# LN2's output behind evacuations, a Wo inside MLP2, and two more groups with all 18 pairs of W2 rows in seven products

## The chip, the cores and the metric

The kernel runs on one core of a Trainium2 chip. The metric is device time in microseconds, the median of three runs; for the kernel before it is 359.16 us (359.07 to 359.28). The engines are called as in the profile: PE (matmuls; PEld is its weight loads), DVE (vector), ACT (scalar and activation), POOL (GpSimd) and SP (here it only issues transfers).

## The reference

One transformer block over 2048 tokens of width D = 576, in bf16. The attention is local: each token looks at W = 8 positions with a step of 2, in 32 heads of 18 columns. The MLP is 4608 wide.

```python
def _A_ref(x, wqkv, wo):
    W, dil = 8, 2
    q, k, v = qkv[0], qkv[1], qkv[2]          # of x @ wqkv, in 32 heads
    idx = pos[:, None] - off[None, :]         # off = arange(W) * dil
    mask = idx >= 0
    logits = jnp.einsum("bhsd,bhswd->bhsw", q, kg) * scale
    logits = jnp.where(mask[None, None, :, :], logits, -1e9)
    attn = _softmax(logits, axis=-1)
    o = jnp.einsum("bhsw,bhswd->bhsd", attn, vg)
    return o @ wo

def _B_ref(x, w1, b1, w2, b2):
    y = _layernorm(x, axis=-1)
    h = _gelu(jnp.einsum("bsd,df->bsf", y, w1) + b1)
    return jnp.einsum("bsf,fd->bsd", h, w2) + b2

h = x + _A_ref(_layernorm(x, axis=-1), A_wqkv, A_wo)
h2 = h + _B_ref(_layernorm(h, axis=-1), B_w1, B_b1, B_w2, B_b2)
```

## The kernel before, in words

**Tiles and stages.** The tokens are 16 tiles of 128 rows (token = 16 * row + tile), so that a tile's window lies in tiles of the same parity. First comes LN1 and QKV for all tiles, in 24 "visits" of two products each (the loop over `qd`). A visit works on 64 partitions at a time: phase 0 of each product in it, then phase 1 of each, each followed by an evacuation from PSUM on ACT (`qkv_duo`, L316). Three PSUM pairs take turns for these products. Then the tiles go through the rest as eight groups of two (`GROUPS`, here group 0 to 7; the loop over `k`). A group's step has MLP1 (four visits; gelu on ACT, L580, into `h_all`), then MLP2, and around it the Wo, LN2 and attention of later groups: `c, d` are the two tiles of the next group, `e, f` those of the group behind it.

**Order.** The order on each engine is the order in which the program is written (`manual_schedule`): nothing is moved by a scheduler. Lists of functions say what is put where: `after` and `between` (by visit, behind its evacuations), `m1` (ahead of a visit of MLP1), `ia`, `ib` (ahead of a row of MLP2 in groups 0 and 1) and `x` (at a named step of MLP2 in groups 2 to 7).

**Attention** is DVE's: `att_qk_a` (L346, QK products), four additions (L355), `att_max`, the exponential on ACT (`att_exp`, L389), `att_den`, `att_pv_a` (L403, PV products) and its sums (L409, L410). Its output goes back into `q_all`; SP stores it (`dma_out`, `td`) and reads it back turned as `oT` (L441), the Wo's operand. `halo` reloads one tile's rows of K or V shifted by one row, between the tiles.

**LN2.** `ln2_h` (L469, DVE) adds x to Wo's result in PSUM, `ln2_act` computes mean and variance on ACT (L491 to L493), a power on POOL (L494) gives the reciprocal root, `ln2_send` writes the output (L174), and SP stores it and reads it back turned as `hnT` (L510), MLP1's operand. Group 0's two tiles do it inside QKV: statistics on DVE, `ln2_rstd` on POOL (L161), `ln2_norm` on ACT (L535, L174), `h_tail` on POOL, `tr_h` on PE with a cast on ACT (L553).

**MLP2.** Groups 0 and 1 run 36 rows of W2 in two halves of 288 columns for each tile (`mlp2`, L599). Groups 2 to 7 take the two tiles and a pair of rows as a 2 by 2 product of blocks and run it in seven products instead of eight (`mlp2_fast`, `PRODUCTS`, L689). There are 18 pairs (`NM`). The seven need sums of h (`h_sums`, L669: s0 to s3, of 12 pairs at once and of the others behind) and of W2 (`w2_sums`, L659, once). Groups 2 to 5 do so for 16 pairs and run pairs 16 and 17 in eight products (`plain`); groups 6 and 7 run all 18 in seven. The order of steps is a list:

```python
if rows < NM:
    steps = ["wo", "hc", (1, all_), "b", "h", "e", (7, lo), (2, all_), (6, all_), "6", "7", "d", "11", (7, hi), "rest", "in",
              (5, all_), "f", "exp", (4, all_), "21", "22", "o1", "4", (3, all_), "12", "o0", "3"]
```

A tuple is a product over pairs; "b", "d" and "f" are copies from bank to bank on ACT (L776); "o1" are two additions on DVE (L720) that empty two banks, of which MLP1 of the next group uses the first for its second product; the other names run the functions of `x` under that name. `ln2_h` of `c` stands in "hc", that of `d` at the head of "h".

**Where sums lie.** Sums that don't fit in place stand in rows of `q_all`, `x_all` and the K and V rings that are free by then: `t_slot` for W2, `s_slot` for h. The second ring is free only from group 6 on.

Of the kernel before, what the change touches and what calls it, by code (L numbers as in the profile page):

```python
# [11 lines left out]
BF16 = mybir.dt.bfloat16  # L12
# [5 lines left out]
def kernel(  # L18
# [216 lines left out]

    def visit(makes, hook=None, between=(), late=None, apart=False):
# [17 lines left out]
        for n in range(len(makes) + (late is not None)):  # L254
            if late is not None and n == len(makes) - 1:
                first(late)
# [361 lines left out]
    def t_slot(t, m0, m1):  # L618
        if t == 2:
            return w2_block(0, 1, m0, m1).bitcast(F16)  # L620
        i = (0, 1, None, 2)[t]
        if m0 >= 16:
            return ring_blocks(1, (2 * i + m0 - 16) * HALF, m1 - m0, HALF)
        if i == 2 and m0 < 16:
            return ring_blocks(0, RING_T + m0 * HALF, m1 - m0, HALF)
        part = 0 if m1 <= 8 else 1 if m1 <= 12 else 2
        rows, j0 = ((x_all, (1, 9, 13)[part]), (q_all, (4, 12, 0)[part]))[i]
        m = m0 - (0, 8, 12)[part]
        j = j0 + 2 * (m // 2)
# [6 lines left out]
    spare = [False]  # L636
    RING_T = 3 * SR * P

    def s_slot(t, m0, m1):
# [5 lines left out]
        if not ring1_free[0]:  # L645
            rows, j = ((q_all, 15), (x_all, 10), (x_all, 8))[i] if spare[0] else (q_all, 15 - 2 * i)
            return rows[:, j, (m0 - SR) * P:(m1 - SR) * P].bitcast(F16).rearrange("p (m c) -> p m c", c=P)
        return ring_blocks(1, 6 * HALF + (i * (NM - SR) + m0 - SR) * P, m1 - m0, P)

# [57 lines left out]
    def mlp2_fast(g, rows, tags, wo, hooks):  # L707
        last, summed = wo is None, rows < NM
        q, p, r, s = tags
# [50 lines left out]
        }  # L760
        if rows < NM:
            steps = ["wo", "hc", (1, all_), "b", "h", "e", (7, lo), (2, all_), (6, all_), "6", "7", "d", "11", (7, hi), "rest", "in",
# [38 lines left out]
    with tc.manual_schedule(engines={ENG.PE, ENG.Activation, ENG.DVE, ENG.SP, ENG.Pool}):  # L801
# [132 lines left out]
        for v, fns in ((2, [(load_w1, 0)]), (3, [(load_w1, 1)]), (4, [(load_w1, 2)]), (6, [(load_wo, [0])]), (8, [(load_wo, [1, 2])]),  # L934
# [68 lines left out]

        def mlp1(grp, plan, ahead, between, late=None):
            for v, duos in enumerate(plan):
                call(ahead.get(v, ()))
                visit([mlp1_duo(grp, us, tag) for us, tag in duos], None, between.get(v, ()), late if v == 3 else None)

# [18 lines left out]

        ROWS = {6: NM, 7: NM}
        p, q, r, s = "ABDC"

        gelu_table()
        for k, g in enumerate(GROUPS):
            c, d = GROUPS[k + 1] if k + 1 < len(GROUPS) else (None, None)
            e, f = GROUPS[k + 2] if k + 2 < len(GROUPS) else (None, None)
            m1, mid, ia, ib, late_wo = {0: []}, {}, {}, {}, None
            if k in (1, 2):
# [7 lines left out]
            if k == 0:  # L1044
# [11 lines left out]
            elif k == 1:  # L1056
                m1[0] += [c_(att_pv_sum, d), c_(send_o, d), c_(halo, d, 2)]
                m1[1] += [c_(att_qk_a, e), c_(halo, e, 1), c_(read_o, d), c_(att_qk_b, e, 0), c_(halos, 7)]
                m1[3] += [c_(out_store, GROUPS[0][0]), c_(att_qk_a, f), c_(halo, f, 1), c_(att_qk_add, f, ((0, 0, 9), (0, 0, 4)))]
                ia[0] = [c_(wo_visit, (c, "B"), (d, "C")), c_(ln2_pair, c, d), c_(att_qk_b, f, 1, 2), c_(att_max, (e, f)),  # L1060
                         c_(exps, e, f), c_(w2_sums, 0, 8, (0, 1)), c_(w2_sums, 8, 12, (0, 1)), c_(att_den, e, f)]
                ia[2] = [c_(pv_sum, e), c_(dma_tr_o, e), c_(reload_x, GROUPS[4])]
                ib[0] = [c_(finish_out, g[0]), c_(out_sum, g[0])]
            if k < 2:
                mlp1(g, mlp1_plan(p, q, r, s, (s, r, p) if k else (r, s, p)), m1, mid, late_wo)
                mlp2_tile(g, 0, "D", ia)
                mlp2_tile(g, 1, "C", ib)
                continue
            rows = ROWS.get(k, 16)
            spare[0] = k == 2  # L1070
# [84 lines left out]
```

## Time and profile before

| | before |
|---|---|
| median of three runs | 359.16 us |
| profiled execution | 359.3 us, span 357.5 us |
| granted PE clock | 1.000 |
| busy in the span: PE, DVE, ACT, POOL | 351.9, 298.5, 235.8, 48.4 us |
| QKV ends, MLP1 of group 0 begins | 65.4 us |
| MLP1, Wo and MLP2 of group 3 | 177.7 to 213.6 us |
| MLP2 of group 4, of group 5, of group 6 begins | 233.6, 269.4, 305.2 us |

Times are from the start of the span. A timeline line has the start, the length, the engine, the line of the kernel, the operation, what it writes and reads, and the number of instructions that it merges; a bracket at its end is the idle time of the engine ahead of it and what ended that. A line of the waits has the waiter, what it waited for, the sum, the number of times and the longest. SPq is SP issuing a transfer, which lands later.

### The profile page before, as it was taken

How to read it: one execution, taken by the hardware profiler on the slowest of the kernel's cores; microseconds unless marked ns; L12 is line 12 of the kernel's file. 1: busy time of each engine (PE TensorE's matmuls, PEld its weight loads, DVE VectorE, ACT ScalarE, POOL GpSimd, SP SyncE). 2: the span in 40 equal slices, each digit the busy share in tenths (PEclk: the TensorE clock that was granted, in tenths of full speed). 3: DMA queues.
4: the chain of work that ended last, by engine and by line, in shares of the span. 5: the costliest groups of instructions: out<-in, count | busy, mean ns of one | idle time of the engine just before them, and what ended most of it. 6: DMA issues, size and time to landing. Idle time of an engine off the chain costs nothing.

```text
span 357.5 us, 11586 instructions
## 1 busy us (share of the span) xinstructions
PE 351.9 (98%) x4945; PEld 291.5 (82%) x4945; DVE 298.5 (84%) x428; ACT 235.8 (66%) x524; POOL 48.4 (14%) x63
## 2 busy tenths in 40 slices
PE   8999999999999999999999999999999999999996
PEld 4777987998788877887788778877887788778874
DVE  5999999999989999999999989998999998520431
ACT  4889756996647683678566856695669566706620
POOL 2241004000212020201200220022002200210000
PEclk9999999999999999999999999999999999999999
DMA  7997799954847584732553455345535253262001
GB/s 240 332 293 169 182 255 295 388 189 87 206 72 123 162 227 76 132 72 51 100 99 85 109 108 80 89 103 112 84 88 103 62 88 51 58 130 37 4 1 34
DMA packets 63492, 46.29 MB, mean 129 GB/s; under 512 B 32192, under 2 KB 61760, under 8 KB 63440
## 3 DMA queue, kind: packets, MB, share of 16 engines
q1 hardware_dynamic: 59472, 41.50, 44.1%
q0 software_dynamic: 3744, 3.84, 9.8%
q8 instruction: 38, 0.62, 0.7%
q10 hardware_dynamic: 224, 0.22, 0.3%
q14 instruction: 14, 0.11, 0.1%
HBM read 23.38 MB, written 12.42 MB: 100 GB/s over the span
## 4 chain that ended last, share of the span: by engine, by line
PE 51%; DVE 39%; ACT 3%; issue 2%; DMA 2%; SPq 1%; POOL 0%; DVEq 0%; POOLq 0%; ACTq 0%
PE pm L222 24%; PE po L689 24%; DVE prod L355 7%; DVE prod L346 6%; DVE prod L403 6%; DVE prod L409 5%; DVE ln_stats L148 3%; PE pw L222 3%; DMA x_all<-in_A_x_dram 1%; DVE den L397 1%; DVE h L469 1%; ACT h_all L580 1%; SPq L104 1%; DVE peak L370 1%; DVE q_all L410 1%
## 5 line engine op out<-in xcount | busy, mean ns | idle before, releaser
L222 PE MATMUL pm<-hnT,w_sb 64*128 64x256 bf16 x2304 | 143.0, 269 | 0.0
L580 ACT ACTIVATE h_all<-pm,b_sb 128x256 f16<-128x256 f32 (+1 forms) x288 | 108.6, 496 | 51.0 <-PE pm L222 50.4
L222 PEld LDWEIGHTS <-w_sb 64*128 64x128 bf16 x2304 | 113.2, 94 | 13.8 <-issue 1.6
L222 PE MATMUL pq<-wq_sb,xnT 64*128 64x288 bf16 x720 | 54.9, 283 | 1.0 <-ACT kv_ring L316 0.5
L689 PEld LDWEIGHTS <-h_all 128*128 128x128 f16 x464 | 44.7, 98 | 13.4 <-issue 1.8
L222 PEld LDWEIGHTS <-xnT 64*128 64x128 bf16 x864 | 43.7, 94 | 10.4 <-issue 1.4
L355 DVE TENSOR_TENSOR prod<-prod 128x2304 bf16<-128x2304 bf16 (+1 forms) x64 | 44.2, 691 | 2.1
L403 DVE TENSOR_TENSOR prod<-kv_ring,probs 128x4608 bf16<-128x4608 bf16 x16 | 40.9, 2558 | 0.9 <-DMA kv_ring<-kv_dram 0.4
L346 DVE TENSOR_TENSOR prod<-kv_ring,q_all 128x4608 bf16<-128x4608 bf16 x16 | 40.9, 2556 | 0.8 <-POOL ln_rstd L494 0.4
L222 PE MATMUL pm<-hnT,w1h_sb 64*128 64x256 bf16 x288 | 39.5, 269 | 0.0
L409 DVE TENSOR_TENSOR prod<-prod 128x2304 bf16<-128x2304 bf16 (+1 forms) x32 | 33.9, 1058 | 1.1
L689 PE MATMUL po<-w2a_sb,h_all 128*128 128x288 bf16 (+1 forms) x252 | 34.2, 286 | 0.2 <-ACT po L776 0.2
L599 PEld LDWEIGHTS <-h_all 128*128 128x128 bf16 x288 | 27.9, 98 | 7.9 <-issue 0.9
L689 PEld LDWEIGHTS <-kv_ring 128*128 128x128 f16 x252 | 24.7, 98 | 6.2
L599 PE MATMUL po<-w2a_sb,h_all 128*128 128x288 bf16 x224 | 28.5, 286 | 0.0
L789 POOL DMA_DIRECT2D x_all<-o_sb x12 | 10.7, 890 | 125.9 <-PE pw L222 54.4
L222 PE MATMUL pq<-wqh_sb,xnT 64*128 64x288 bf16 x144 | 27.6, 283 | 0.0
L494 POOL TENSOR_TENSOR ln_rstd<-ln_var,mhalf 128x1 f32<-128x1 f32 x13 | 10.3, 795 | 78.2 <-ACT ln_var L493 78.2
L669 DVE TENSOR_TENSOR kv_ring<-h_all 128x1536 f16<-128x1536 f16 (+3 forms) x9 | 6.8, 753 | 15.9 <-ACT h_all L580 15.9
L222 PE MATMUL pw<-wo_sb,oT 64*128 64x288 bf16 x256 | 19.5, 283 | 0.0
L161 POOL TENSOR_TENSOR ln_rstd<-ln_veps,mhalf 128x1 f32<-128x1 f32 (+2 forms) x14 | 13.1, 949 | 45.8 <-DVE ln_nmean L483 28.3
L689 PE MATMUL po<-w2b_sb,h_all 128*128 128x288 bf16 (+1 forms) x112 | 18.8, 286 | 0.2 <-DVE h_all L669 0.2
(121 smaller groups left out, 410.2 us busy)
## 6 DMA issues: line engine op xcount, KB each, us to landing
w_sb<-in_B_w_dram SPq DMA_DIRECT2D x6, 768.0 KB, 6.8
kv_ring<-kv_dram SPq DMA_DIRECT2D x28, 144.0 KB, 2.4
kv_dram<-kv_ring SPq DMA_DIRECT2D x13, 288.0 KB, 3.2
w2a_sb<-in_B_w_dram SPq DMA_DIRECT2D x3, 1008.0 KB, 9.7
x_all<-in_B_b_dram SPq DMA_DIRECT2D x15, 144.0 KB, 4.3
td<-q_all SPq DMA_DIRECT2D x14, 144.0 KB, 1.8
td<-hn SPq DMA_DIRECT2D x14, 144.0 KB, 1.8
x_all<-h POOLq DMA_DIRECT2D x14, 144.0 KB, 4.8
```

Source lines behind the costliest of these rows:

```text
L148: nc.vector.bn_stats(out=stats[:, i, c, :], in_=src[:, c * HALF:(c + 1) * HALF])
L161: nc.gpsimd.tensor_tensor(out=rstd[:], in0=veps[:], in1=mhalf[:].to_broadcast([P, n]), op=ALU.pow)
L222: last = nc.tensor.matmul(duo["g"][r ^ swap][i], lhsT=lhsT, rhs=rhs, start=(swap == 0 and i == 0 and kt == 0), stop=(swap == 1 and kt == K ...
L346: ins = nc.vector.tensor_tensor(out=prod[:], in0=k_ring[j % 2], in1=q_all[:, j, :].unsqueeze(1) .to_broadcast([P, W, D]), op=ALU.mult).ins
L355: nc.vector.tensor_tensor(out=prod[:, :, o * H:o * H + n], in0=prod[:, :, a * H:a * H + n], in1=prod[:, :, c * H:c * H + n], op=ALU.add)
L403: nc.vector.tensor_tensor(out=prod[:].rearrange("p w (d h) -> p w d h", h=H), in0=v_ring[j % 2].rearrange("p w (d h) -> p w d h", h=H), in ...
L409: nc.vector.tensor_tensor(out=prod[:, 0:n, :], in0=prod[:, 0:n, :], in1=prod[:, n:2 * n, :], op=ALU.add)
L494: ins = nc.gpsimd.tensor_tensor(out=rstd[:], in0=var[:], in1=mhalf[:], op=ALU.pow).ins
L580: pace[0] = nc.scalar.activation(out=hT(grp)[:, f, 0:N], in_=ps[:, r, i * N:(i + 1) * N], func=ACT.Gelu_apprx_tanh, bias=b1_sb[:, f:f + 1] ...
L599: nc.tensor.matmul(banks[half], lhsT=hT(grp)[:, f, i * P:(i + 1) * P], rhs=w2_rows(f)[:, half * HALF:(half + 1) * HALF], start=(f == 0), s ...
L689: nc.tensor.matmul(bank, lhsT=l, rhs=r, start=start, stop=stop, skip_group_check=True)
L789: nc.gpsimd.dma_start(out=x_of(j), in_=o_of.pop(j), accum_op=ALU.add)
```

## The change

It has five parts.

1. In QKV, the root, output and tail of LN2's first tile move by a visit or a place, so that on ACT two more evacuations stand ahead of its output; the exponential of group 1's first tile moves from visit 22 behind the evacuations of visit 23.
2. In group 0, the Wo of group 1's first tile is taken out of MLP1's last visit and put at the head of MLP2, cut in two by two rows of MLP2 (`fill`), as the second tile's Wo is; that one moves from row 19 to row 21.
3. In group 1, the second addition of a QK product moves behind the two `ln2_h`.
4. In groups 2 to 4 the sum s2 of 12 pairs moves from ahead of MLP2 into "hc", behind `ln2_h` of the first tile; in group 5 from the head of "h".
5. Groups 4 and 5 run all 18 pairs in seven products. The sums of W2 for pairs 16 and 17 move from group 6 to group 4 and into rows of `q_all`. The sums of h get other places: s1 of pairs 12 to 17 in a new buffer of `hnT` (so the turned LN2 output waits for its readers), s0 and s3 in `homes`. As written, s0 and s3 of pairs 16 and 17 lie in the first 512 columns of the row that holds s3 of pairs 12 to 15 and are written later, so product 3 of groups 4 and 5 reads other values there; the number, kind and order of instructions does not hang on that. The rows of x for group 6 are fetched in group 4 behind product 3 instead of in group 3.

```diff
@@ mlp2_fast
-        last, summed = wo is None, rows < NM
+        last, summed = wo is None, g not in GROUPS[6:]
...
-        if rows < NM:
+        if summed:
@@ t_slot, pairs 16 and 17
-            return ring_blocks(1, (2 * i + m0 - 16) * HALF, m1 - m0, HALF)
+            return q_all[:, 15 - 2 * i, (m0 - 16) * HALF:(m1 - 16) * HALF].bitcast(F16).rearrange("p (m c) -> p m c", c=HALF)
@@ s_slot
+    step_of, top = [0], [None]
+    homes = {2: ((q_all, 15), (x_all, 10), (x_all, 8)), 3: ((q_all, 15), (q_all, 13), (q_all, 11)), 4: ((q_all, 9), (x_all, 4), (x_all, 6)),
+             5: ((q_all, 9), (q_all, 5), (q_all, 7))}
...
-            rows, j = ((q_all, 15), (x_all, 10), (x_all, 8))[i] if spare[0] else (q_all, 15 - 2 * i)
+            if step_of[0] in FULL and t == 1:
+                rows, c = top[0][:].rearrange("p k c -> p (k c)"), 0
+            else:
+                rows, j = homes[step_of[0]][2 if m0 >= 16 else i]
+                rows, c = rows[:, j, :], (16 - SR - i) * P if m0 >= 16 else 0
...
+    def new_top():
+        top[0] = sb.tile([P, KT, 2 * P], BF16, tag="hnT", name="hnT")
@@ between, the visits of QKV
-            20: [c_(h_tail, A[0])],
-            19: {0: [c_(ln2_rstd, A[0])], 1: [c_(ln2_norm, A[0])]},
-            21: {0: [c_(ln2_rstd, A[1])], 1: [c_(ln2_norm, A[1])]},
-            22: {0: [c_(tr_h, A[0], "D")], 1: [c_(h_tail, A[1]), c_(att_exp, A[2])]},
+            19: [c_(ln2_rstd, A[0])],
+            20: {1: [c_(ln2_norm, A[0])]},
+            21: {0: [c_(h_tail, A[0]), c_(ln2_rstd, A[1])], 1: [c_(ln2_norm, A[1])]},
+            22: {0: [c_(tr_h, A[0], "D")], 1: [c_(h_tail, A[1])]},
+            23: {1: [c_(att_exp, A[2])]},
@@ group 0
-                late_wo = wo_duo(c, "B")
-                ia[0] = [c_(ln2_h, c), c_(ln2_act, c), c_(put_b2, c), c_(halos, 2), c_(ln2_send, c), c_(att_qk_b, e, 0)]
-                ia[19] = [lambda d=d: wo_visit((d, "A"), fill=True), c_(ln2_h, d), c_(ln2_act, d), c_(put_b2, d), c_(ln2_in, c),
+                ia[0] = [lambda c=c: wo_visit((c, "B"), fill=True), c_(ln2_h, c), c_(ln2_act, c), c_(put_b2, c), c_(halos, 2), c_(ln2_send, c), c_(att_qk_b, e, 0)]
+                ia[21] = [lambda d=d: wo_visit((d, "A"), fill=True), c_(ln2_h, d), c_(ln2_act, d), c_(put_b2, d), c_(ln2_in, c),
@@ group 1
-                m1[3] += [..., c_(att_qk_add, f, ((0, 0, 9), (0, 0, 4)))]
-                ia[0] = [c_(wo_visit, (c, "B"), (d, "C")), c_(ln2_pair, c, d), c_(att_qk_b, f, 1, 2), c_(att_max, (e, f)),
+                m1[3] += [..., c_(att_qk_add, f, ADDS[:1])]
+                ia[0] = [c_(wo_visit, (c, "B"), (d, "C")), c_(ln2_pair, c, d), c_(att_qk_b, f, 1, 1), c_(att_max, (e, f)),
@@ groups 2 to 7
-        ROWS = {6: NM, 7: NM}
+        FULL = (4, 5, 6, 7)
...
-                early = (0,) if k == 5 else (0, 2)
-                m1[3] += [c_(h_sums, 0, min(rows, SR), early)]
-                if k == 5:
-                    x["h"] += [c_(h_sums, 0, SR, (2,)), c_(h_sums, 0, SR, (1, 3))]
-                else:
-                    x["h"] += [c_(h_sums, 0, SR, [t for t in range(4) if t not in early])]
-                x["h"] += [c_(h_sums, SR, rows)]
+                m1[3] += [c_(h_sums, 0, SR, (0,))]
+                x["hc"] += [c_(h_sums, 0, SR, (2,))]
+                x["h"] += [c_(h_sums, 0, SR, (1, 3))]
+                if k in FULL:
+                    x["h"] += [new_top]
+                x["h"] += [c_(h_sums, SR, 16)]
+                if k in FULL:
+                    x["h"] += [c_(w2_sums, 16, NM)] if k == FULL[0] else []
+                    x["h"] += [c_(h_sums, 16, NM)]
...
-                    m1[1].append(c_(w2_sums, 16, NM))
...
-            if k + 3 < len(GROUPS):
-                x["3" if k == 2 else "in"] += [c_(reload_x, GROUPS[k + 3])]
+            if k in (2, 4):
+                x["3"] += [c_(reload_x, GROUPS[5 if k == 2 else 6])]
+            if k == 4:
+                x["in"] += [c_(reload_x, GROUPS[7])]
```

More of the change, by code (lines that the diff above doesn't have):

```diff
@@ L234, in marker, with visit @@
         return nop
-    def visit(makes, hook=None, between=(), late=None, apart=False):
+    def visit(makes, hook=None, between=(), apart=False):
         duos, marks = [], []
@@ L253, in visit @@
             return
-        for n in range(len(makes) + (late is not None)):
-            if late is not None and n == len(makes) - 1:
-                first(late)
+        for n in range(len(makes)):
             phase(duos[n], 1, marks[n])
@@ L635 @@
     ring1_free = [False]
-    spare = [False]
+    step_of, top = [0], [None]
+    homes = {2: ((q_all, 15), (x_all, 10), (x_all, 8)), 3: ((q_all, 15), (q_all, 13), (q_all, 11)), 4: ((q_all, 9), (x_all, 4), (x_all, 6)),
+             5: ((q_all, 9), (q_all, 5), (q_all, 7))}
     RING_T = 3 * SR * P
@@ L645, in s_slot @@
         if not ring1_free[0]:
-            rows, j = ((q_all, 15), (x_all, 10), (x_all, 8))[i] if spare[0] else (q_all, 15 - 2 * i)
-            return rows[:, j, (m0 - SR) * P:(m1 - SR) * P].bitcast(F16).rearrange("p (m c) -> p m c", c=P)
-        return ring_blocks(1, 6 * HALF + (i * (NM - SR) + m0 - SR) * P, m1 - m0, P)
+            if step_of[0] in FULL and t == 1:
[3 more added lines that the diff above has]
+                rows, c = rows[:, j, :], (16 - SR - i) * P if m0 >= 16 else 0
+            return rows[:, (m0 - SR) * P - c:(m1 - SR) * P - c].bitcast(F16).rearrange("p (m c) -> p m c", c=P)
+        return ring_blocks(1, (i * (NM - SR) + m0 - SR) * P, m1 - m0, P)
+    def new_top():
+        top[0] = sb.tile([P, KT, 2 * P], BF16, tag="hnT", name="hnT")
     def h_block(odd, i, m0, m1):
@@ L1002, in mlp1_plan, with mlp1 @@
             return [[([2 * v + n], tag) for n, tag in enumerate(tags)] for v, tags in enumerate(((p, q), (r, s), (p, q), end))]
-        def mlp1(grp, plan, ahead, between, late=None):
+        def mlp1(grp, plan, ahead, between):
             for v, duos in enumerate(plan):
                 call(ahead.get(v, ()))
-                visit([mlp1_duo(grp, us, tag) for us, tag in duos], None, between.get(v, ()), late if v == 3 else None)
+                visit([mlp1_duo(grp, us, tag) for us, tag in duos], None, between.get(v, ()))
         def mlp2_tile(grp, i, tag, inserts):
@@ L1034 @@
             e, f = GROUPS[k + 2] if k + 2 < len(GROUPS) else (None, None)
-            m1, mid, ia, ib, late_wo = {0: []}, {}, {}, {}, None
+            m1, mid, ia, ib = {0: []}, {}, {}, {}
             if k in (1, 2):
@@ L1058 @@
                 m1[1] += [c_(att_qk_a, e), c_(halo, e, 1), c_(read_o, d), c_(att_qk_b, e, 0), c_(halos, 7)]
-                m1[3] += [c_(out_store, GROUPS[0][0]), c_(att_qk_a, f), c_(halo, f, 1), c_(att_qk_add, f, ((0, 0, 9), (0, 0, 4)))]
-                ia[0] = [c_(wo_visit, (c, "B"), (d, "C")), c_(ln2_pair, c, d), c_(att_qk_b, f, 1, 2), c_(att_max, (e, f)),
+                m1[3] += [c_(out_store, GROUPS[0][0]), c_(att_qk_a, f), c_(halo, f, 1), c_(att_qk_add, f, ADDS[:1])]
+                ia[0] = [c_(wo_visit, (c, "B"), (d, "C")), c_(ln2_pair, c, d), c_(att_qk_b, f, 1, 1), c_(att_max, (e, f)),
                          c_(exps, e, f), c_(w2_sums, 0, 8, (0, 1)), c_(w2_sums, 8, 12, (0, 1)), c_(att_den, e, f)]
@@ L1064 @@
             if k < 2:
-                mlp1(g, mlp1_plan(p, q, r, s, (s, r, p) if k else (r, s, p)), m1, mid, late_wo)
+                mlp1(g, mlp1_plan(p, q, r, s, (s, r, p) if k else (r, s, p)), m1, mid)
                 mlp2_tile(g, 0, "D", ia)
@@ L1068 @@
                 continue
-            rows = ROWS.get(k, 16)
-            spare[0] = k == 2
+            rows = NM if k in FULL else 16
+            step_of[0] = k
             x = {n: [] for n in ("hc", "h", "6", "7", "in", "exp", "4", "3")}
```

## The prediction

> **What bounds the kernel now.** I read the page's shares and chain first, then the waits of PE, the chain in order of time, and the timelines of the engines at each place that the change touches.
>
> ```profile
> PE 351.9 (98%) x4945; PEld 291.5 (82%) x4945; DVE 298.5 (84%) x428; ACT 235.8 (66%) x524; POOL 48.4 (14%) x63
> PE 51%; DVE 39%; ACT 3%; issue 2%; DMA 2%; SPq 1%; POOL 0%; DVEq 0%; POOLq 0%; ACTq 0%
> ```
>
> PE works nearly all the time and DVE almost as much. The waits of PE, all that the profile has of them behind the first microseconds:
>
> ```profile
> PE pq L222 <- ACT kv_ring L316: 0.5, 1, 0.5
> PE po L689 <- ACT po L776: 0.2, 1, 0.2
> ```
>
> From about 165 us the chain is PE alone. Its pieces (start, length) give the price of a group's MLP1, Wo and MLP2, with 128 and with 126 products:
>
> ```profile
> 213.58 17.79 PE pm L222 x324
> 231.37 2.21 PE pw L222 x36
> 233.58 15.79 PE po L689 x128
> ...
> 305.15 15.54 PE po L689 x126
> ```
>
> So the end moves by what PE's work and its stalls become, and DVE counts where something that PE needs comes late. DVE's timeline in groups 4 to 7 shows how little it has to spare; the bracket is idle time and what ended it:
>
> ```profile
> 232.08 0.96 DVE L669 TENSOR_TENSOR h_all<-h_all 128x1536 f16<-128x1536 f16 x1
> 233.13 1.42 DVE L469 TENSOR_TENSOR h<-pw,x_all 128x576 f32<-128x576 f32 x2
> 239.28 2.56 DVE L346 TENSOR_TENSOR prod<-kv_ring,q_all 128x4608 bf16<-128x4608 bf16 x1 [0.44 <-POOL ln_rstd L494]
> 247.01 0.95 DVE L720 TENSOR_TENSOR o_sb<-po,o_sb 128x288 f32<-128x288 f32 x2 [0.44 <-PE po L689]
> 260.30 0.46 DVE L410 TENSOR_TENSOR q_all<-prod 128x576 bf16<-128x576 bf16 x1
> 268.91 1.42 DVE L469 TENSOR_TENSOR h<-pw,x_all 128x576 f32<-128x576 f32 x2 [1.08 <-PE pw L222]
> 296.85 0.45 DVE L659 TENSOR_TENSOR kv_ring<-w2b_sb 128x576 f16<-128x576 bf16 x1
> 342.02 0.29 DVE L669 TENSOR_TENSOR kv_ring<-h_all 128x256 f16<-128x256 f16 x1 [1.36 <-ACT h_all L580]
> ```
>
> The last things that PE waits for from DVE are the attention outputs: SP stores them and reads them back turned as oT for the Wo of the same group. SP's issues, the page's time to landing, and PE's second Wo in groups 5 and 6:
>
> ```profile
> 262.84 1.21 SPq L441 DMA_TRANSPOSE oT<-td  x1
> 298.94 1.21 SPq L441 DMA_TRANSPOSE oT<-td  x1
> oT<-td SPq DMA_TRANSPOSE x14, 2.9
> 267.60 0.65 PE L222 MATMUL pw<-wo_sb,oT 64*128 64x288 bf16 x8
> 303.39 0.65 PE L222 MATMUL pw<-wo_sb,oT 64*128 64x288 bf16 x8
> ```
>
> Landed at 262.84 + 2.9 = 265.7 and 298.94 + 2.9 = 301.8, the outputs lie ready 1.9 us and 1.6 us ahead of PE. That is the margin that a later DVE may use up.
>
> **The change part by part.**
>
> *LN2 output and exponential behind evacuations.* At 58.20 PE has two products left and would go on at 58.32; it goes on at 58.95, because ACT first waited 1.75 us for POOL's power (54.28 to 57.14), wrote LN2's output (0.29 + 0.87) and only then emptied the bank (58.27, 0.63). With two evacuations ahead of that output the bank is empty at about 57.6, and 0.63 us go. What is late next: the output of the second tile keeps its place, it hangs on DVE (h at 58.76, power until 61.61), so the evacuation behind it still ends at 63.37; PE's next user of that bank began at 63.51 and can begin at 63.42 at best. Of 0.63 us 0.09 are left. Then MLP1 began at 65.44, right behind the cast of hnT (64.69 to 65.39), which had the exponential (0.43) ahead; without it the cast can begin at 64.4, ends at 65.1, and PE begins at 65.16. Gain 0.28, which holds the 0.09. The exponential moves behind both evacuations (to about 66.2) and pushes the table load (1.28) by as much; the first gelu had 0.71 us of idle time ahead of it, and the softmax sum needs it at 70.5. Nothing.
>
> *Wo in MLP2.* The Wo of group 1's first tile stood inside MLP1's last visit with one change from its products on 64 rows to MLP2's on 128 (pw to po at 84.34). Now it is cut in two within MLP2, as the second tile's is: at 88.9 to 91.05 such a cut costs 0.17 into Wo and 0.16 out of it, start to start beyond the plain pace (0.0545 us a product on 64 rows by pairs, 0.122 on 128). The new cut adds one more way in, with 0.14 + 0.07, and one more way out, 0.16: +0.36. Bounds: nothing, if the array were free in between, and 0.69, twice the whole. I take 0.36, the row of the same cut. Its h on DVE starts at 87.5, behind a QK product; Wo is then done at about 85. The second tile's Wo moves two rows (four products, 0.49) later; h at 91.62 waits some 0.1 us, which DVE loses.
>
> *One addition less ahead of group 2's h's.* DVE's h's of 124.78 start about 0.5 us earlier and LN2 on ACT with them; the addition of 0.70 is done behind. The exponentials come sooner and DVE's idle 0.76 us at 133.6 goes.
>
> *h's ahead of sums.* In group 2, PE's 12 products from 163.36 would end in a next start at 164.83; it was 165.24, for the copy of a bank (164.79, 0.39) behind ACT's statistics, which waited 0.85 for h at 162.10. Now h goes ahead of a 0.96 us sum; ACT is then held by its own gelus until 162.04, the copy starts at 164.1, and 0.41 us go. The sum itself still comes at 162.7, where product 7 wants it at 163.4. In group 3 and 4 PE waits for nothing there, and DVE loses: between the first sum's end (232.04) and Wo's result (233.13) it did the second sum; now it idles there and does the sum behind h, a step of 0.87 us more. In group 3 an idle 0.90 ahead of o_sb at 211.23 covers this. In group 4 the next item uses that cover.
>
> *All 18 pairs in groups 4 and 5.* PE: 126 for 128 products, 15.79 − 15.54 = 0.25 a group, −0.50. DVE in group 4 does the four sums of W2 (296.85 to 298.65, steps 0.48 + 0.48 + 0.39 + 0.37 = 1.72; they leave group 6, where DVE waits anyway) and in both groups four sums of h of 0.29 (steps 0.33 + 0.21 + 0.20 + 0.21 = 0.95). Group 4: 0.87 + 1.72 + 0.95 = 3.54 more; of the idle 0.44 and 0.44 all but the usual 0.03 each, so 0.82, is used up: DVE ends the group 2.72 us late. Bounds for this lag: 1.5, if each sum cost the shortest step of its kind (4 x 0.37 + 4 x 0.20 - 0.82) and h's idle time did not arise, and 3.5, if no idle time were recovered; I take 2.72, as every step has its own row. Product 6 needs its last sums at 241.42 and gets them at about 241.1; MLP1's second bank is emptied at 250.2, when PE wants it: up to 0.08 lost.
>
> *The lag at PE.* Group 5's attention is DVE without a gap, so its second output ends at 260.76 + 2.72 = 263.48, is issued 2.08 later and lands 2.9 behind that, at 268.46. PE, 0.17 early by then (0.25 less 0.08), wants it at 267.43: a stall of 1.03. This covers the sum that product 7 needs (272.2). In group 5 h comes late too, at 266.95 + 2.72 + 0.92 = 270.59 for 268.91; with four small sums more DVE passes on 1.68 + 0.95 = 2.63 us into group 6, whose second output lands at 301.84 + 2.63 = 304.47. PE wants it at 303.39 − 0.17 + 1.03 − 0.25 = 304.00: 0.47 more. Behind it DVE idles 1.73 us (h at 304.70) and the lag is gone; the last two groups run as before. Stalls 0.08 + 1.03 + 0.47 = 1.58.
>
> *x reloads and POOL.* The rows of group 6 are fetched behind group 4's product 3 instead of in group 3. SP's next issues there wait for DVE anyway (252.83), and the rows are needed at 270: nothing, and if that cover were gone, the fetch's 3.6 us would delay the halo and add to the lag. The turned LN2 outputs now wait for product 6, at 241.7; SP issued them at 242.51.
>
> Sum: −0.28 + 0.36 − 0.41 − 0.50 + 1.58 = **+0.75 us**. The profiled execution took 359.3 (span 357.5, 1.8 around it), 0.14 above the median of 359.16; against the median the forecast is 359.9.
>
> **The rivals.**
>
> *The lag stays hidden (faster).* Place: oT of groups 5 and 6. If DVE's lag is below 1.6 us there, no output is late, and the sum is −0.28 + 0.36 − 0.41 − 0.50 = −0.83, 358.3. For it: 1.5 as the lower bound of the lag. Against it: the sums' rows vary by hundredths. It decides at 1.6 us.
>
> *A slow transfer falls on the late one (slower).* The oT of 262.84 took 4.6 us to land, where the median is 2.9; the margin hid it. With none, 4.6 − 2.9 = 1.7 go to PE in full: 361.6. The longest of the 14 took 4.9; two are exposed. In the window of 262 to 268 the instruction queue (q8) fetched its one 16 KB packet. [...]
>
> *The early gains don't come.* If the stalls at 58.95 and 165.24 only move on, +0.69 is left out: 360.6. For it: the first moves by my own working. I count it within the forecast's range.
>
> **How the numbers follow.** Forecast 0.55 (its own range 359.4 to 360.6), hidden lag 0.15, slow transfer 0.25, something else 0.05. A measurement of this kernel can tell about 0.2% (0.72 us) from no change. The forecast lies on that bound: 0.30 slower, 0.24 same, 0.01 faster. Hidden lag: 0.10 faster, 0.05 same. Slow transfer: slower. The rest: 0.03 slower, 0.02 same. Together 0.11, 0.31, 0.58. Range 358.4 to 361.7: from the hidden lag to the slow transfer.
>
> **What would show it.** A second Wo in groups 5 and 6 that starts 0.3 to 1.2 us behind its first, with PE waiting for oT; h of group 5 at 1.5 us or more behind its Wo; no wait at 58.95 and 165.24; the Wo of group 1 in two pieces; o_sb of group 4 some 2.7 us later than now. If DVE's lag in group 5 is under 1.6 us, or PE's Wo shows no wait there, the forecast is wrong.

## The result, and the profile after

The changed kernel takes 361.69 us in the median of 22 runs (359.62 to 364.46), the kernel before 359.16 (358.60 to 361.38, 22 runs): ratio 1.0058, 95% interval 1.0045 to 1.0071. It is slower, by 0.6%. Its times fall into two heaps: seven runs at 359.6 to 360.2, fifteen at 361.4 to 364.5. The profiled execution (360.0, span 358.2) is of the first heap; a second profile, shown below, is of the other.

The page of the changed kernel, busy times and chain:

```profile
PE 351.0 (98%) x4941; PEld 289.2 (81%) x4941; DVE 299.6 (84%) x436; ACT 235.8 (66%) x524; POOL 47.5 (13%) x63
...
q8 instruction: 38, 0.62, 0.8%
...
PE 70%; DVE 15%; DMA 6%; ACT 4%; SPq 2%; issue 2%; DVEq 0%; ACTq 0%
```

q8 is read here as the queue that brings PE's instructions: 38 blocks of 16 KB for 9,882 of them (PE and PEld, 4,941 each), of which the one near group 5's store comes at the same place of PE's program in all fourteen traces (see e5). PE has 0.9 us less work than before; DVE has 1.1 us more, and transfers have 6% of the chain for 2%. Behind QKV, PE's waits (waiter, cause: sum, times, longest) have two new lines:

```profile
PE pm L222 <- DMA hnT<-td: 0.8, 1, 0.8
...
PE pw L222 <- DMA oT<-td: 0.6, 1, 0.6
```

The first is ahead of group 5's MLP1, the second ahead of the second Wo of group 6; from start to start of PE's products they cost 0.91 and 0.76 us beyond the usual step. Against the profile of before:

| | forecast | profiled execution |
|---|---|---|
| PE ahead at the end of group 3's MLP2 (212.80 for 213.30) | -0.33 | -0.50 |
| 126 for 128 products, groups 4 and 5 (15.54 each) | -0.50 | -0.50 |
| wait for LN2's turned output, group 4's step | 0 | 0.91 |
| bank at 250.2; second Wo of group 5 | 0.08; 1.03 | 0; 0 |
| second Wo of group 6 | 0.47 | 0.76 |
| sum; span | +0.75 | +0.67; +0.7 |

Why LN2's output was late stands in SP's timeline, first of the kernel before, then of the changed one (start, length):

```profile
240.88 0.43 SPq L205 DMA_DIRECT2D td<-hn  x1
241.87 0.33 SPq L341 DMA_DIRECT2D kv_ring<-kv_dram  x1
242.51 2.52 SPq L510 DMA_TRANSPOSE hnT<-td  x2
```

```profile
240.36 0.43 SPq L205 DMA_DIRECT2D td<-hn  x1
244.37 0.33 SPq L339 DMA_DIRECT2D kv_ring<-kv_dram  x1
244.88 2.52 SPq L508 DMA_TRANSPOSE hnT<-td  x2
```

The stores went out earlier than before, but a refill of the K ring stands ahead of the turned reads in SP's queue. It waits until DVE's QK product has read the ring (SP waited 3.5 us for it, and issued the refill 0.03 us behind its end at 244.34), and DVE was late. DVE of the changed kernel:

```profile
241.79 2.55 DVE L344 TENSOR_TENSOR prod<-kv_ring,q_all 128x4608 bf16<-128x4608 bf16 x1
```

That is 2.51 us later than the 239.28 of before. The chain of the changed kernel at group 6 shows the other wait (start, length, what): store, turned read, Wo, each straight behind the one before.

```profile
299.49 1.54 DMA td<-q_all
...
301.11 2.93 DMA oT<-td
...
304.08 1.77 PE pw L222 x26
```

### The profile page after: what moved, and what is told of

Read it like the earlier page. It is cut to its first block, busy times and chain, and to the rows that moved or that the text cites. A ratio compares the mean times of both kernels' runs of the same rounds, so it can differ in the third digit from the quotient of the medians.

```text
span 358.2 us, 11596 instructions
## 1 busy us (share of the span) xinstructions
PE 351.0 (98%) x4941; PEld 289.2 (81%) x4941; DVE 299.6 (84%) x436; ACT 235.8 (66%) x524; POOL 47.5 (13%) x63
## 4 chain that ended last, share of the span: by engine, by line
PE 70%; DVE 15%; DMA 6%; ACT 4%; SPq 2%; issue 2%; DVEq 0%; ACTq 0%
PE pm L222 29%; PE po L696 16%; PE pq L222 11%; PE po L597 10%; PE pw L222 3%; DVE prod L353 2%; ACT h_all L578 2%; DVE prod L401 2%; DVE prod L344 2%; DVE prod L407 2%; DMA xnT<-xd 2%; DMA td<-q_all 2%; DMA x_all<-in_A_x_dram 1%; SPq L104 1%; DVE kv_ring L676 1%
## 5 line engine op out<-in xcount | busy, mean ns | idle before, releaser
L696 PEld LDWEIGHTS <-h_all 128*128 128x128 f16 x448 | 43.3, 98 | 12.6 <-issue 1.4
L222 PEld LDWEIGHTS <-xnT 64*128 64x128 bf16 x864 | 42.0, 94 | 12.3 <-issue 1.4
L783 ACT COPY po<-po 128x288 f32<-128x288 f32 x17 | 6.6, 386 | 18.8 <-PE po L696 18.8
```

The lines of the kernel that those rows point to most:

```text
L222: last = nc.tensor.matmul(duo["g"][r ^ swap][i], lhsT=lhsT, rhs=rhs, start=(swap == 0 and i == 0 and kt == 0), stop=(swap == 1 and kt == K ...
L696: nc.tensor.matmul(bank, lhsT=l, rhs=r, start=start, stop=stop, skip_group_check=True)
```

## The experiments

The kernel before took 359.07 to 359.19 us in the same sessions; a ratio is against it. W2's sums are those of `w2_sums`, s2 is the sum of 12 pairs that the change moved.

### e1_again: the other heap

The changed kernel, no edit.

> The changed kernel, unaltered, profiled a second time. Its 22 times fall into two heaps, seven at 359.6 to 360.2 us and fifteen at 361.4 to 364.5; the profile at hand (360.0) shows the short heap, with PE waiting 0.91 us for the turned LN2 output in group 4's step and 0.83 us for the second attention output of group 6. Theory 1, a slow transfer: a profile of the long heap shows the same waits and one of them some 2 us longer, by a landing of over 4 us where the short one has 2.4 to 3.7. Theory 2, DVE itself runs slower in the long heap (its instructions longer or with more gaps): then DVE's chain from 210 us on is some 2 us longer and every wait behind it grows. Theory 3, the start: the first transfers come 2 us later. If the run falls into the short heap the profile repeats the one at hand within 0.3 us.

361.62 us. PE's waits:

```profile
PE pw L222 <- DMA oT<-td: 2.6, 2, 1.7
...
PE pm L222 <- DMA hnT<-td: 0.7, 1, 0.7
```

Beyond the usual step they are 0.80 (LN2), 1.81 (Wo of group 5, where the short profile has none) and 1.09 (Wo of group 6). The chain at group 5's second output:

```profile
262.36 0.34 SPq L204
...
262.75 3.37 DMA td<-q_all
...
266.17 2.83 DMA oT<-td
...
269.05 1.03 PE pw L222 x13
```

The store took 3.37 us; the read behind it took its usual 2.8. The transfers from 263 to 267, in 40 slices of 0.1 us (busy share in tenths, then GB/s):

```profile
DMA  0069993636000000000001000000000000000000
GB/s 0 0 242 415 392 323 105 104 49 164 0 0 0 0 0 0 0 0 0 0 4 6 0 0 0 0 0 0 0 0 0 0 0 0 0 0 0 0 0 0
...
q8 instruction: 1, 0.02, 1.7%
```

The packets of the two stores run from 263.2, those of the small one (issued at 262.75) from 263.7. In the tenth slice one 16 KB block of instructions begins (the 164; it is booked at its start, 264.00, and took 1.07 us). Then nothing, and at 265.0 to 265.2 the last few small packets. Packet by packet: 120 of the small store's 128 had gone by 263.91, the other eight, a sixteenth of them where the profile counts 16 DMA engines, began at 265.05, when the block was through; which engine a packet took, the trace does not show. The short profile, 263.5 to 267.5:

```profile
DMA  0189974720000005000000000025477999732000
GB/s 0 69 311 380 380 265 99 107 28 0 0 0 0 0 0 164 0 0 0 0 0 0 0 0 0 0 51 125 118 164 179 259 243 225 172 62 42 0 0 0
```

Here the store is through at 264.39 and the block begins at 265.08, between the store and the turned read. So theory 1 holds, a transfer, though in the small store and not in the read; DVE's instructions around it have the same lengths in both (theory 2 falls), and up to group 5 the long execution is 0.44 us ahead (247.90 for 248.34), so theory 3 falls too.

### e2_sp_order: turned reads ahead of the refill

```diff
-                x["in"] = [c_(ln2_ins, c, d)] + x["in"]
+                if k == 4:
+                    x["7"].insert(1, c_(ln2_ins, c, d))
+                else:
+                    x["in"] = [c_(ln2_ins, c, d)] + x["in"]
```

> One edit to the changed kernel: in group 4's step SP issues the two turned reads of LN2's output ahead of the K ring's refill that waits for DVE's QK product (it ended at 244.34 us in the profile; the stores had landed at 241.94 and product 6 was over). Both theories say that the reads are issued at about 242.0 instead of 244.9, land by about 246.5, and PE's wait of 0.91 us ahead of group 5's MLP1 is gone. Theory A, DVE's chain sets the end from group 4 to 6: DVE's outputs come no sooner, PE arrives 0.9 us earlier at Wo of group 5 and waits some 0.3 us there (output landed at 267.69, PE would want it at 267.35), and the rest again at group 6 (landed at 304.04): the time stays at that of the changed kernel within 0.2 us. Theory B, the order on SP is the whole loss: the waits at Wo stay as they were and the time falls by 0.9 us, to 359.1 for a run like the profiled one. The rarer and the commoner heap of times (360 and 362) may change their shares: if the long heap comes from the late turned read, it is gone here and the median falls below 360.2.

362.29 us in six runs (361.46 to 362.52), ratio 1.0082 (1.0066 to 1.0097). SP's timeline and PE's largest wait:

```profile
241.67 2.52 SPq L508 DMA_TRANSPOSE hnT<-td  x2
244.29 0.53 SPq L339 DMA_DIRECT2D kv_ring<-kv_dram  x1
```

```profile
PE pw L222 <- DMA oT<-td: 2.1, 1, 2.1
```

The wait for LN2's output is gone, as both theories said, and nothing is won: PE comes sooner to Wo of group 5 and waits there. Theory B falls. Theory A had the time stay within 0.2 us, and it is 0.6 above; PE's granted clock, the page's row of 40 slices in tenths, shows what came on top:

```profile
PEclk9999999999999999999999999999998999999999
```

PE's step ahead of that Wo was 2.39 us. From 270.25 on the granted clock was 0.5 for 3.41 us; the rest of the Wo took 2.41 us for 1.69 and MLP2 16.46 for 15.54, so the stall cost 1.6 us more than its wait. (A further 0.4 us is a wait for POOL's markers in group 5's MLP1.) In e1_again a step of 1.94 us left the clock at 1.0.

In this profile, too, eight packets of the store stayed back until 265.38, when a block (264.45) was through; its record begins 0.43 us behind the last of the other 120, so the eight were late before it begins, which the block's record does not explain. No run was in the short heap.

### e3_s2_ahead, e7_no_w2_sums, e10_no_lag: less work on DVE in group 4

```diff
@@ e3: s2 of group 4 ahead of Wo again
-                m1[3] += [c_(h_sums, 0, SR, (0,))]
-                x["hc"] += [c_(h_sums, 0, SR, (2,))]
+                m1[3] += [c_(h_sums, 0, SR, (0, 2) if k == 4 else (0,))]
+                if k != 4:
+                    x["hc"] += [c_(h_sums, 0, SR, (2,))]
@@ e7: no W2's sums for pairs 16 and 17 (e10: both edits)
-                    x["h"] += [c_(w2_sums, 16, NM)] if k == FULL[0] else []
```

> One edit to the changed kernel: in group 4 alone the sum s2 of 12 pairs stands ahead of MLP2 again, as in the kernel before; it fills 0.96 of the 1.07 us in which DVE waited for Wo at 231.56. Theory A, DVE's chain sets the end: all that DVE does behind it comes 0.9 us earlier (the QK product at 240.9 instead of 241.79, the second output of group 6 landed at 303.1 instead of 304.04), PE's wait for the turned LN2 output falls from 0.91 to under 0.1 us, and the time falls by 0.9 us, to 359.1 for a run like the profiled one; PE's waits left are some 0.8 us, at Wo of group 6. Theory B, the lag of DVE counts for little and the order on SP for all: the time still falls by 0.9 us, but the wait at Wo of group 6 stays at 0.83 us with its output landed at 304.0. In group 4 the copy of a bank behind ACT's statistics may cost PE up to 0.1 us.

> The changed kernel with the four sums of W2 for pairs 16 and 17 left out altogether (products 4 to 7 of the last four groups read other values for these pairs), which takes 1.72 us of DVE out of group 4. Theory A, DVE's lag is what PE waits for: the waits of 0.91 us (turned LN2 output of group 4) and 0.83 us (second attention output of group 6) both go, and a short run takes 358.3 us; a block of instructions on the store of group 5's second output delays it to about 267.9 where PE wants it at 267.35, so a long run takes 358.9. Median 358.3 to 358.9. If instead the new buffer of s1 or the order on SP holds the turned LN2 output, the wait ahead of group 5's MLP1 stays at some 0.9 us and the time stays above 359.2.

> Both of DVE's additions that could be taken away alone: the sum s2 ahead of MLP2 in group 4 and the four sums of W2 left out altogether (products 4 to 7 of the last four groups read other values for pairs 16 and 17). DVE then has 0.95 us more in group 4 than with the first four parts alone, and 0.82 of idle time to take it. Each edit alone gave 360.28 and 359.18 us. If DVE's lag, and the blocks of instructions that fall on its late outputs, are all that part 5 loses, the 2 x 0.25 us of PE now show in full: no wait at group 5's MLP1 and at Wo of groups 5 and 6, 358.67 - 0.50 = 358.2 us. If a block of instructions still reaches the turned read of group 6 (it took 2.9 to 4.3 us so far), PE waits there for up to 0.5 us: 358.7. If part 5 costs something that isn't DVE's (the new homes, the later fetch of x), the time stays at 358.9 or more with a wait elsewhere.

| run | DVE's lag less by | median us (runs) | range | ratio, interval |
|---|---|---|---|---|
| e3_s2_ahead | 0.96 | 360.28 (12) | 358.51 to 361.69 | 1.0027, 1.0010 to 1.0044 |
| e7_no_w2_sums | 1.72 | 359.18 (12) | 358.36 to 361.59 | 1.0001, 0.9986 to 1.0017 |
| e10_no_lag | both | 359.44 (11) | 358.83 to 360.13 | 1.0010, 0.9998 to 1.0021 |

Each edit alone takes the wait for LN2's output away, with SP's order and the new buffer as they were: the lag of DVE made it (theory A). The profile of e3 was its fastest run, 358.51, and PE's waits behind QKV are down to Wo of group 6:

```profile
PE pw L222 <- DMA oT<-td: 0.5, 1, 0.5
```

What its other runs wait for, no profile shows. The medians don't follow the lag down. e7 lies 0.3 us above its expectation and e10 no lower than e7, where I expected 358.2 or, with a block on the read, 358.7. In e10 the chain at group 6 is

```profile
298.42 4.46 DMA oT<-td
...
302.93 0.29 PE pw L222
```

The read went out 2.7 us sooner than in the changed kernel, and took 4.46 us for 2.93. Of its 32 completion writes 30 were done by 300.82; a block began at 300.88, and the last two came at 301.82. In e7 the read was issued 0.81 us later than in e10 (299.23) and landed only 0.30 us later (303.18). PE's wait at this Wo, which e7 was to lose, was 1.26 us beyond the usual step in e7 and 0.97 in e10, for 0.76 in the changed kernel: PE came there sooner, the output did not. In e10 the landing (302.88) followed the last two writes, behind a block that comes with PE's own program, and of the 2.7 us by which the read went out sooner 1.16 were left (304.04 in the changed kernel).

### e5_block_later, e9_block_earlier, e13_no_lag_block_later: where the blocks fall

In all fourteen traces, q8's block near group 5's store comes when PE has begun 7,603 to 7,644 of its 9,900 instructions: a place in PE's program, give or take half a microsecond. These edits move that place and nothing behind the start.

```diff
@@ e5, and e13 (on top of e10)
-        for n in [512] * 8 + [P] * 8:
+        for n in [512] * 9:
...
-        for n in range(12):
+        for n in range(10):
@@ e9
-        for n in [512] * 8 + [P] * 8:
+        for n in [512] * 6 + [P] * 16:
```

> The changed kernel with 9 fewer warm-up products at the very start (9 of 512 columns instead of 8 of 512 and 8 of 128; 10 small ones instead of 12), which are 18 instructions of PE less, and nothing else. The traces so far: q8 fetches one 16 KB block of instructions per some 256 instructions of PE. In the long profile (361.6) the block began at 264.00, as the small second store of group 5's second attention output ended (120 of its 128 packets by 263.91); its last 8 packets started at 265.05, when the block was through, and the turned read behind it was issued at 266.17 instead of 264.81. In the short profile (360.0) the block began at 265.08, 0.69 us behind the store's end, and no packet was held. Theory C, the block on the store makes the long heap: 18 instructions fewer put the block some 0.5 us later against all else (256 instructions lasted 7.5 us there), past the store in nearly all runs; the long heap is gone or rare and the median falls from 361.7 to 359.9 to 360.6 (the block may touch the turned read of group 6, 0.5 us at most). Theory D, the heaps have another cause (the state of the chip, DVE): the times fall into the same two heaps, about two in three at 361.4 or more, median near 361.7.

> The other way: 6 warm-up products more (6 of 512 and 16 of 128 columns, about the same time), 12 instructions of PE more, so that each 16 KB block of instructions is fetched some 0.35 us earlier against all else. Theory C, the block on the store makes the long heap: the short heap needs the block to start more than 0.4 us behind the store's end, so it becomes rarer still, at most one run in six, and the median stays at 361.7 to 362.4. Theory D, another cause: seven of 22 in the short heap as before.

> The run with s2 ahead in group 4 and without W2's sums (359.44 us), with 18 instructions of PE fewer in the warm-up, so that each 16 KB block of instructions comes some 0.5 us later. There the block of 300.88 held the last two of the 32 completion writes of group 6's turned read (30 by 300.82, two at 301.82), which landed at 302.88, and PE waited 1.05 us in the fastest kind of run. Theory C: the block comes behind that read in most runs, the wait falls below 0.3 us and the time to 357.9 to 358.6, so that the 0.5 us of PE's fewer products show. Against it: that PE, with fewer products, meets the read of group 6 before it has landed whatever the block does; then the time stays at 359.2 or more, and the profile shows the wait with a landing of 2.9 us or less.

e5: 360.46 us in ten runs, eight of them at 360.2 to 360.7; ratio 1.0039 (1.0024 to 1.0054). That is within theory C's 359.9 to 360.6, though between the two heaps and not in the short one. The profiled one is the longest, 361.9. Its block comes at 266.20, behind the store's end at 265.13, and the store is free; but the next block lies on group 6's read, and the chain there is

```profile
301.60 4.35 DMA oT<-td
```

e9: 360.89 us in seven runs (360.49 to 362.02), ratio 1.0051 (1.0033 to 1.0069). None is in the short heap, as theory C said, but the median was to be 361.7 or more. In its profile the block (263.67) holds the store as in e1_again, and lets it go earlier, so that the store takes less:

```profile
262.68 2.98 DMA td<-q_all
```

These two ran one after the other on one chip, the 22 runs of the changed kernel at another time, so the shares of the heaps are best compared between the two. The step from e5 to e9 goes in the direction of theory C, and is smaller than it said: that packets stay back until a block is through is seen in the traces (eight of 128 in e1_again, e2 and e9), how much of the heaps it makes is in part argued.

e13: 359.78 us in twelve runs; eleven of 359.5 or more, one of 357.72; ratio 1.0021 (1.0005 to 1.0038). Neither expectation fits. The block still lies on the read's end: 30 of 32 completion writes by 301.74, the block at 301.90, two writes at 302.83, and the chain

```profile
299.46 4.47 DMA oT<-td
...
303.97 1.03 PE pw L222 x13
```

In e10 and here the block's record begins within 0.02 us of the read's last packet, though it was moved by 18 instructions. Whether the block itself queues behind the read's packets, so that half a microsecond doesn't part them, stays open. The one run at 357.72, 2 us below the rest, would be an execution in which they missed each other; it has no profile, so this is argued only.

### e4_parts1to4, e6_no_cut, e12_sums_only: the first four parts

```diff
@@ e4: groups 4 and 5 as before
-        FULL = (4, 5, 6, 7)
+        FULL = (6, 7)
@@ e6, on top of e4: Wo of group 1's first tile back in MLP1
-                ia[0] = [lambda c=c: wo_visit((c, "B"), fill=True), c_(ln2_h, c), ...]
-                ia[21] = [...]
+                late_wo = wo_duo(c, "B")
+                ia[0] = [c_(ln2_h, c), ...]
+                ia[19] = [...]
@@ e12, on top of e6: LN2 in QKV as before
-            19: [c_(ln2_rstd, A[0])],
-            20: {1: [c_(ln2_norm, A[0])]},
-            21: {0: [c_(h_tail, A[0]), c_(ln2_rstd, A[1])], 1: [c_(ln2_norm, A[1])]},
-            22: {0: [c_(tr_h, A[0], "D")], 1: [c_(h_tail, A[1])]},
-            23: {1: [c_(att_exp, A[2])]},
+            20: [c_(h_tail, A[0])],
+            19: {0: [c_(ln2_rstd, A[0])], 1: [c_(ln2_norm, A[0])]},
+            21: {0: [c_(ln2_rstd, A[1])], 1: [c_(ln2_norm, A[1])]},
+            22: {0: [c_(tr_h, A[0], "D")], 1: [c_(h_tail, A[1]), c_(att_exp, A[2])]},
```

> The changed kernel without its fifth part: groups 4 and 5 run 16 pairs in seven products and two in eight, and the sums of W2 for the last two pairs are back in group 6, in the second ring (only the later fetch of group 6's x stays). By the theory that the fifth part makes all the loss, DVE is late by no more than 0.1 us in group 4 (0.87 more work, 0.82 of idle time to take it), PE waits nowhere from 205 to 305 us, and PE stays as far ahead of the kernel before as it was at 212.8 us in the profile, 0.50 us: 358.8 for a profiled run, ratio about 0.9986, and the long heap is as rare as in the kernel before (4 of 22). By the rival, that the first four parts cost as well (the second addition of group 4's idle place, the cut Wo), the time is 359.2 or more. By my own earlier sum the first four parts are worth 0.28 - 0.36 + 0.41 = 0.33 us.

> The run with the first four parts only (358.67 us), with one edit: the Wo of group 1's first tile is back in MLP1's last visit, in one piece, and the second tile's Wo back at row 19. By my prediction's row the cut costs 0.36 us of changes between products on 64 and on 128 rows (in the profile of the changed kernel 0.155 + 0.098 + 0.07 + 0.155 at 83.5 to 84.7, of which the uncut one has 0.155): the time falls to 358.3. By the rival that DVE, which this Wo releases half a microsecond sooner, gains as much elsewhere, it stays at 358.7 within 0.15 us.

> The kernel before with the third and fourth part alone (the addition behind the h's of group 2, and h's ahead of the sum s2), and the later fetch of group 6's x. By my prediction's terms the first part is worth 0.28 us and these two 0.41, the bank copy that group 2 no longer waits for; with the first, third and fourth together the time was 358.71. If both terms stand this run takes 0.28 us more than that, 359.0, or by its own term 359.16 - 0.41 = 358.75; if the first part's stall only moves on (one profile has 0.595 us at 62.3 where the kernel before had 0.689 at 58.2 and 0.243 at 65.1), it takes 358.7 to 358.8.

The later fetch of group 6's rows of x stays in all three.

| run | parts | median us (runs) | ratio, interval |
|---|---|---|---|
| e4_parts1to4 | 1, 2, 3, 4 | 358.67 (12) | 0.9982, 0.9972 to 0.9993 |
| e6_no_cut | 1, 3, 4 | 358.71 (12) | 0.9988, 0.9977 to 1.0000 |
| e12_sums_only | 3, 4 | 358.59 (11) | 0.9986, 0.9977 to 0.9994 |

All three lie together, e4 and e12 with intervals below 1: they beat the kernel before by 0.5 us and the changed one by 3.0. So part 5 alone costs 361.69 - 358.67 = 3.0 us. The profile of the short heap shows 0.91 + 0.76 - 0.50 = 1.2 of it, that of the other heap 0.80 + 1.81 + 1.09 - 0.50 = 3.2. The gain is that of parts 3 and 4; the cut Wo and the moved LN2 change nothing that these runs can tell. PE's waits of e12, all of them, and the chain through groups 2 to 6, which is PE alone:

```profile
PE busy L838 <- PEq L1152: 0.8, 1, 0.8
PE pq L222 <- DMA xnT<-xd: 0.2, 1, 0.2
```

```profile
161.17 15.79 PE po L698 x128
176.96 17.79 PE pm L222 x324
```

MLP2 of group 2 runs through in 15.79 us; the wait of 0.41 for a bank is gone, and nowhere behind it does PE wait.

### e11_sums_on_pool: W2's sums on POOL

e10 with the four sums done on POOL, ahead of the second visit of group 4's MLP1.

```diff
-                nc.vector.tensor_tensor(out=out, in0=a, in1=b, op=ALU.subtract)
+                eng.tensor_tensor(out=out, in0=a, in1=b, op=ALU.subtract)
...
+                if k == FULL[0]:
+                    m1[1].append(c_(w2_sums, 16, NM, range(4), nc.gpsimd))
```

> The same with the four sums of W2 done after all, on POOL, early in group 4 (ahead of the second visit of MLP1), where POOL has nothing else to do: the whole computation of the changed kernel. If POOL takes nothing from DVE, the time is that of the run without these sums, 358.2 us or 358.7. If the two engines hold each other up when both read, DVE loses up to POOL's busy time: the four sums cost DVE 1.80 us (296.85 to 298.65 in the kernel before), and if POOL takes that from it the time is that of the run with s2 ahead alone, 360.3.

365.20 us in five runs (364.69 to 366.01), ratio 1.0181 (1.0165 to 1.0197): a miss on all sides. PE's largest wait, and POOL's timeline:

```profile
PE pm L222 <- POOLq L232: 4.1, 1, 4.1
```

```profile
217.63 2.27 POOL L666 TENSOR_TENSOR q_all<-w2b_sb,q_all 128x576 f16<-128x576 bf16 x1
223.18 1.62 POOL L666 TENSOR_TENSOR q_all<-w2b_sb,q_all 128x576 f16<-128x576 bf16 x1 [3.28 <-DMA td<-q_all]
```

POOL had something to do: the markers of a visit (L232), for which PE waits between its two phases, are POOL's instructions, and they stood behind a sum that waited 3.28 us for its row of `q_all` to be stored. PE went on at 223.28. As in e2, the granted clock was then 0.5 for 3.41 us, from 223.84.

## Why the prediction was right, and where it was not

The sign was right. The median lies at the very edge of the range, 361.69 for 361.7, and that it lies inside is luck. The forecast itself, 359.9, describes the profiled execution (360.0) and its heap of seven; the fifteen others are the rival "a slow transfer falls on the late one", at 361.6, to which I gave 0.25.

- **Early parts.** As a sum right: -0.33 forecast, -0.50 in the profile, -0.52 in the runs (e4's 358.67 for 359.19). Singly not: each against the kernel before of its own session, parts 3 and 4 give -0.54 (forecast -0.41), the cut -0.07 (forecast +0.36), part 1 +0.09 (forecast -0.28), the last two within what these runs tell from nothing; that two wrong terms cancel is luck.
- **The cut.** Its price is there in PE's steps at 83.5 to 84.7, at half its size: from MLP1 of group 0 to MLP1 of group 1 PE takes 38.39 us with the cut and 38.20 in e12. In e6, without it, the second tile's Wo waited 0.3 us longer at 89.6.
- **Part 1.** Its stall seems to have moved on: in six profiles (e1, e3, e6, e7, e10, e11) PE waits 0.4 to 0.5 us for an evacuation at 62.9 to 63.3, where the kernel before waited at 58.95. In the six others with part 1 neither stall shows, but PE had waited up to 1.3 us earlier in QKV, mostly for transfers, and e12, without part 1, doesn't show the stall at 58.95 either. So what part 1 is worth stays open.
- **A wait left out.** Part 4 also acts where I wrote that "PE waits for nothing there": the list of PE's waits that I showed lacks `PE po L689 <- DVE h_all L669: 0.2, 1, 0.2`, which stood ahead of group 3's MLP2 (Wo 2.45 us from start to start, 2.30 after, 2.35 in e12).
- **Products.** 15.54 us in both groups, as forecast.
- **DVE's lag.** 2.72 forecast; DVE entered group 4 0.48 us sooner (213.98 for 214.46) and left it 2.04 later (249.91 for 247.87), so 2.52.
- **The lag at PE.** 1.58 forecast, 0.91 + 0.76 = 1.67 in the short heap. The size held, as the lag sets when group 6's output lands (304.04, forecast 304.47) wherever PE waits before; the place did not. The step that failed is "The turned LN2 outputs now wait for product 6, at 241.7; SP issued them at 242.51", costed at nothing: I moved DVE by 2.72 us but left SP where it was, although the refill ahead of those reads waits for DVE's QK product, which my own lag puts at 244.6 (it ended at 244.34). e2 agrees that this changes where PE waits and wins nothing, though there a block on the store lengthened the later wait. The margin of 1.9 us at group 5 goes by the median landing of 2.9 us; the read of 262.84 itself landed at 267.48 in that trace, 0.12 us ahead of PE.
- **The slow transfer.** The step that failed is its chance, which I took from how many landings were slow among fourteen. It isn't drawn by lot: this block comes at one place of PE's program (7,603 to 7,644 instructions begun, in fourteen traces), so a transfer that stands there can be met in most executions (15 of 22 here, if all are like the one profiled). The size, 1.7, held (1.81 at group 5); the transfer was the small store ahead of the read, which the prediction left out. The trace of before had shown the block at 265.44, at the end of that read's packets.
- **The instruction blocks.** The changed kernel's trace has 38 for 9,882 instructions of PE, and PE's list of waits names none of them. The packets beside one were late: in e1_again eight of the store's 128 began only at 265.05, when the block that began at 264.00 and took 1.07 us was through.
- **Hidden lag** (358.3). No run of the changed kernel came under 359.62.

## What to carry to other kernels

Where a second engine is nearly as busy as the one that sets the time (DVE 84%, PE 98% here), work saved on the first is worth only the margin that the second's outputs have, and work added to the second must be followed through every queue that waits for it, the transfers' too. A transfer with no margin should be counted at its slow length (4.46 us in e10 for 2.93) if a block of instructions passes near it in the trace, since here that came at nearly the same place in all fourteen traces. A stall behind which PE's clock falls costs more than its wait (1.6 us more in e2), so the granted clock belongs in the account of each long wait. Of a change in several parts, run the parts: two of these five gave the 0.5 us, and one took 3.0.

## What the runs showed of the hardware

A 16 KB block of instructions takes 0.9 to 2.6 us, 1.07 in the median of 532 blocks in fourteen traces. In five of the traces a sixteenth of a transfer's packets stayed back until a block was through: 8 of a store's 128 in e1_again, e2 and e9, 2 of a read's 32 completion writes in e10 and e13. There the landing came 0.9 to 1.1 us behind the last packet (265.24 to 266.12 in e1_again, 301.85 to 302.88 in e10, 302.86 to 303.93 in e13), and 0.3 to 0.4 behind it in the changed kernel's profile, where no block stood at the end of the transfer (264.40 to 264.78, 303.75 to 304.04).

After a step of 2.39 us in PE's products (e2) and one of 4.34 (e11), the granted clock was 0.5 for 3.41 us; after steps of 1.94 (e1_again) and 1.83 (e5) it stayed at 1.0.

POOL's sums of 128x576 took 1.62 to 2.38 us, and two of DVE's additions, beside the sums of 223.18 and 224.76, were longer than elsewhere. DVE's timeline in e11_sums_on_pool:

```profile
223.70 4.06 DVE L407 TENSOR_TENSOR prod<-prod 128x2304 bf16<-128x2304 bf16 x2
```

These two (2.31 and 1.72) take 1.36 and 0.76 elsewhere. Each took 0.95 us more, though the first is elsewhere 1.8 times as long as the second, so they were not slowed in proportion to their length; what held them no run shows.
